# The first batch of an FFT filter takes the path of the later batches, through DRAM

## The chip, the cores and the metric

The kernel runs on one core of one Trainium2 chip. The metric is the device time of one execution in microseconds; the time given for a kernel is the median of its runs. TensorE multiplies matrices into PSUM, VectorE (DVE), ScalarE (ACT) and GpSimd (POOL) work elementwise, and nearly all transfers are issued by SyncE, whose queue (SPq) takes its instructions strictly in order.

## The reference

```python
X = np.fft.rfft(x, axis=1)                       # x: (8, 3072, 256) float32
y = np.fft.irfft(X * (filt_r + 1j*filt_i), n=3072, axis=1)
t = y.reshape(8*3072, 256)
h = np.maximum(t @ w_in, 0.0)                    # w_in (256, 2048), w_out (2048, 256): float64
z = h * h @ w_out
logits = z @ phi                                 # 32 slots = 8 experts x 4
slots = softmax(logits, over tokens).T @ z       # per expert: relu(slots @ w1) @ w2
out = softmax(logits, over slots) @ slots_out    # (24576, 256) float32
```

## The kernel before

The FFT of length 3072 is 128 x 24. Stage A multiplies the 128-point matrix with all of a batch (12 units of 128 x 512); its result S has to be regrouped, so that the 24-point matrices of stage B meet 24 values of one frequency block on the partitions. After stage B comes the filter (a complex product), then the inverse 24-point products, whose result G lies in DRAM. Each 512-token chunk is then read back from G (`gin`), takes the inverse 128-point product (line 408), is split in two halves of precision (`xo`, line 434) and goes through the pairs of the main loop: lines 468 to 470 multiply it with `wiH` and `wiL`, the two halves of w_in. There are 384 pairs, and TensorE is busy nearly all the time in them.

Work is ordered by hand. Each step is a function with a time, `put(t, fn)`; the times are only sort keys. Before the main loop there is a start stage: everything in `ev0`, sorted, fired in that order. In the main loop four streams (`dsp`, `late`, `fft`, `w`) are merged with the pairs by their times, so batches 1 to 7 transform beside the pairs of the batch before them.

Batches 1 to 7 use `fft_events`: S goes to DRAM (`S<-u`, 12 stores of 256 KB) and comes back regrouped in 8 rounds of two loads (`f<-S`, each 192 KB into 48 partitions, one at partition 0, one at 64). A round has 16 products of 48 x 32 by 256 (line 181; the trace counts them as 32), four VectorE products with the filter (line 192), four GpSimd sums (line 201), 16 inverse products (line 214), four copies out of PSUM on ScalarE (line 223) and two stores to G.

Batch 0 uses `start_events`. It keeps S on chip and regroups it by transfers from SBUF to SBUF: in each of 16 rounds two transfers `bi<-S` (line 324) read 4 partitions of S, 24 KB each, and write 96 partitions, 1 KB each. A round then has two 96 x 128 products (line 331), the filter in three VectorE operations and one sum, two inverse products (line 351), a copy (line 357) and a store `G<-go` (line 361). It has constants and a filter layout of its own (`fwf`, `ivf`, `pkf`), and half of each filter tile is copied from the other half on ScalarE (line 318).

The start stage also turns w_in, which comes as 8 float64 blocks, into `wiH` and `wiL`: per block a load `wt<-w_in`, a ScalarE copy (line 677), five VectorE operations (lines 649 to 654 and 688), a ScalarE copy to `wiH` (line 691) and a GpSimd difference `wiL` (line 693). Blocks of w_out are turned in the same way in the first pairs of the main loop. When the start stage ends, `open_main` gives its SBUF and PSUM to the main loop.

The framework gives SPq's transfers 8 completion semaphores in turn, so a transfer is not issued before the eighth before it has landed.

Of the kernel before, what the change touches and what calls it, by code (L numbers as in the profile page):

```python
# [38 lines left out]
def body(tc, x, cA, cAf, fwd, inv, flt, fwf, ivf, pkf, cst, w_in, w_out, phi, w1, w2, out):  # L39
# [26 lines left out]

    def groups(g):
        return [ST["B0"] + 1.2 + ST["dB"] * (g + k) for k in (0, 1, 1, 2, 3, 4, 5, 6)]

    WI = ((.35, conv_at(8.4, 0, SEQ, (4.2, 4.3))), (.55, conv_at(12.3, 0, SEQ, (5.6, 5.6))),  # L70
          (.75, conv_at(16.2, 0, SEQ, (4.2, 4.3))), (18.5, groups(0)), (28, groups(6)),
          (50.5, conv_at(59, 0, SEQ, (4, 4))), (52.7, conv_at(62.5, 0, SEQ, (4, 4))),
          (57, conv_at(66.2, 0, SEQ, (4, 4))))
    WO = [((64, 66.5, W)[n] if n < 3 else W + 2 * n - 4.5,
# [180 lines left out]


    def start_events(put, st):
        xv = x[0].rearrange("(p n) d -> p n d", n=N2)
        gv = st["G"].rearrange("(i t r) n d -> i (r n) t d", t=2, r=4)
        ca = first.tile([128, 128], F32, name="ca")  # L260
        S = first.tile([128, N2, D], F32, name="S")
        sv = S.rearrange("p n d -> p (n d)")

        wz = cv.tile([128, 512], F32, tag="wx", name="wz", bufs=1)

        def warm(a, n):

            p = side()
            w = a.shape[1]
            for _ in range(n):  # L270
                pe.matmul(p[:, 0:w], a[:, 0:128], a, start=True, stop=True)

        fb = [first.tile([128, 2048], F32, tag=f"fb{k}", name="fb") for k in range(4)]
        gps.memset(fb[3], 0.0)

        def load_ca():
            vec.memset(wz, 0.0)
            sync.dma_start(out=ca, in_=cAf)

        def load_x(sl):  # L280
            if sl % 2 == 0:
                st["x", sl // 2] = fb[sl // 2].rearrange("p (n d) -> p n d", d=D)
            a = 4 * (sl % 2)
            sync.dma_start(out=st["x", sl // 2][:, a:a + 4, :], in_=xv[:, 4 * sl:4 * sl + 4, :])

        def mm_a(u):
            p = side()
            a = 2 * (u % 4)
            pe.matmul(p, ca, st["x", u // 4][:, a:a + 2, :], start=True, stop=True)
            st["a", u] = p  # L290

        def evac_a(u):
            p = st.pop(("a", u))
            o = sv[:, 512 * u:512 * u + 512]
            act.activation(out=o, in_=p, func=ACTF.Copy)

        def load_w(q):
            w = first.tile([96, 4, 2, 128], F32, tag="fw", name="fwq", bufs=2)
            sync.dma_start(out=w, in_=fwf[q])
            st["fw", q] = w  # L300

        def load_v(q):
            w = first.tile([128, 4, 2, 96], F32, tag="iv", name="ivq", bufs=2)
            sync.dma_start(out=w, in_=ivf[q])
            st["iv", q] = w

        def load_f(h):

            f = fb[(h + 3) % 4].rearrange("p (i t c d) -> p i t c d", i=2, t=2, c=2)
            sync.dma_start(out=f[0:48], in_=pkf[2 * h:2 * h + 2, 0:48].rearrange("i p t c d -> p i t c d"))  # L310
            if h == 0:
                for k in range(2):
                    sync.dma_start(out=f[64:112, k, :, 0, :], in_=pkf[k, 64:112, :, 0, :])
            st["f", h] = f

        def copy_f(h):
            f = st["f", h]
            act.activation(out=f[64:112, :, :, 0, :], in_=f[0:48, :, :, 0, :], func=ACTF.Copy)

        def load_s(i):  # L320
            t = first.tile([96, 2, D], F32, tag="bi", name="bi", bufs=4)
            for tt in range(2):
# [2 lines left out]
            st["bi", i] = t

        def mm_b(i):
            t, c = st.pop(("bi", i)), st["fw", i // 4][:, i % 4]
            p = side()
            for tt in range(2):  # L330
                pe.matmul(p[:, tt * D:tt * D + D], c[:, tt, :], t[:, tt, :], start=True, stop=True)
            st["p", i] = p

        def filt(i):
            p = st.pop(("p", i)).rearrange("p (a d) -> p a d", d=D)
            f = st["f", i // 2][:, i % 2]
            u = first.tile([128, 2, D], F32, tag="u", name="u", bufs=2)
            v = first.tile([128, 2, D], F32, tag="v", name="v", bufs=2)
            vec.scalar_tensor_tensor(
                out=v[0:64], in0=p[64:128], scalar=-1.0, in1=f[0:64, :, 1, :], op0=ALU.mult, op1=ALU.mult  # L340
            )
            vec.tensor_tensor(out=v[64:128], in0=p[0:64], in1=f[0:64, :, 1, :], op=ALU.mult)
            vec.tensor_tensor(out=u, in0=p, in1=f[:, :, 0, :], op=ALU.mult)
            (gps if i < 14 else vec).tensor_tensor(out=u, in0=u, in1=v, op=ALU.add)
            st["y", i] = u

        def mm_g(i):
            y, c = st.pop(("y", i)), st["iv", i // 4][:, i % 4]
            p = side()
            for tt in range(2):  # L350
                pe.matmul(p[0:96, tt * D:tt * D + D], c[:, tt, :], y[:, tt, :], start=True, stop=True)
            st["g", i] = p

        def evac_g(i):
            p = st.pop(("g", i))
            o = first.tile([96, 2, D], F32, tag="go", name="go", bufs=3)
            act.activation(out=o, in_=p[0:96].rearrange("p (a d) -> p a d", d=D), func=ACTF.Copy)
            st["go", i] = o

        def store_g(i):  # L360
            sync.dma_start(out=gv[i], in_=st.pop(("go", i)))

        put(0, load_ca)
        put(0.05, warm, wz, 2)
        put(0.05, warm, wz[:, 0:256], 1)
        put(18.2, warm, ca, 16)
        for sl in range(6):
            put(0.1 * sl + 0.2, load_x, sl)
        for q in range(4):
            T = ST["B0"] + 4 * ST["dB"] * q  # L370
            put(0.8 if q == 0 else T - 6.5, load_w, q)
            put(1 if q == 0 else T - 1, load_v, q)
        for h in range(8):
            T = ST["B0"] + 2 * ST["dB"] * h
            put((1.1, 12.1, 19, 21)[h] if h < 4 else T - 7, load_f, h)
            if h:
                put(T - 0.5, copy_f, h)
        for u in range(12):
            put(4.6 + 0.9 * u, mm_a, u)
            put(6.7 + 1.0 * u, evac_a, u)  # L380
        for i in range(16):
            T = ST["B0"] + ST["dB"] * i
            put(max(T - 5, 18), load_s, i)
            put(T, mm_b, i)
            put(T + 1, filt, i)
            put(T + 5, mm_g, i)
            put(T + 6, evac_g, i)
            put(T + 9, store_g, i)
# [867 lines left out]
```

## Time and profile before

| what | value |
|---|---|
| median of 3 runs | 2188.33 us (2185.21 to 2192.13) |
| the profiled execution | 2184.73 us, span 2183.0 us |
| TensorE busy | 2068.9 us, 95% of the span |
| VectorE, ScalarE, GpSimd busy | 1391.4, 895.0, 848.4 us |
| mean granted TensorE clock | 0.968 of full speed |
| moved by DMA | 237.33 MB, mean 109 GB/s |

The span runs from the first to the last instruction of the profiled execution; 1.7 us of its time lie outside. Shares of busy time are means over a start stage, a long main loop and an end stage, which have different limits, so a stage is read in windows of its own.

### The profile page before, as it was taken

How to read it: one execution, taken by the hardware profiler on the slowest of the kernel's cores; microseconds unless marked ns; L12 is line 12 of the kernel's file. 1: busy time of each engine (PE TensorE's matmuls, PEld its weight loads, DVE VectorE, ACT ScalarE, POOL GpSimd, SP SyncE). 2: the span in 40 equal slices, each digit the busy share in tenths (PEclk: the TensorE clock that was granted, in tenths of full speed). 3: DMA queues.
4: the chain of work that ended last, by engine and by line, in shares of the span. 5: the costliest groups of instructions: out<-in, count | busy, mean ns of one | idle time of the engine just before them, and what ended most of it. 6: DMA issues, size and time to landing. Idle time of an engine off the chain costs nothing.

```text
span 2183.0 us, 43936 instructions
## 1 busy us (share of the span) xinstructions
PE 2068.9 (95%) x17950; PEld 1306.3 (60%) x17950; DVE 1391.4 (64%) x2534; ACT 895.0 (41%) x1771; POOL 848.4 (39%) x864
## 2 busy tenths in 40 slices
PE   6569999999999999999999999999999999999987
PEld 3346655665566656665666556656666556666556
DVE  3357666657665666666665666566666666666648
ACT  2134533443345333543345333533345334333335
POOL 2223543343334443543434433533435433332314
PEclk7569999999999999999999999999999999999999
DMA  6453453234314332242314331333324341300479
GB/s 173 114 158 107 143 128 94 77 116 105 95 45 139 93 99 65 96 126 77 100 53 131 98 106 47 114 108 80 97 67 133 99 108 46 109 23 12 129 251 386
DMA packets 142889, 237.33 MB, mean 109 GB/s; under 512 B 13344, under 2 KB 95840, under 8 KB 142688
## 3 DMA queue, kind: packets, MB, share of 16 engines
q1 hardware_dynamic: 142544, 234.39, 36.3%
q8 instruction: 141, 2.31, 0.5%
q14 instruction: 60, 0.49, 0.1%
q0 software_dynamic: 144, 0.13, 0.0%
HBM read 153.73 MB, written 77.59 MB: 106 GB/s over the span
## 4 chain that ended last, share of the span: by engine, by line
PE 84%; DMA 7%; DVE 5%; SPq 2%; issue 2%; ACT 1%; ACTq 0%; DVEq 0%
PE p L468 18%; PE p L470 15%; PE p L469 15%; PE sd L587 10%; PE L L496 8%; PE sd L408 4%; DMA bi<-S 3%; PE sd L181 3%; PE sd L214 2%; DMA f<-S 2%; PE sd L535 2%; DVE h L477 1%; PE sd L141 1%; PE sd L142 1%; PE sd L143 1%
## 5 line engine op out<-in xcount | busy, mean ns | idle before, releaser
L480 POOL TENSOR_TENSOR h<-h 128x512 f32<-128x512 f32 x384 | 399.7, 1041 | 961.6 <-ACT h L479 903.5
L468 PE MATMUL p<-xo,wiH 128*128 128x512 f32 x1536 | 669.3, 436 | 11.3 <-DVE h L477 8.5
L469 PE MATMUL p<-xo,wiH 128*128 128x512 f32 x1536 | 608.4, 396 | 0.9 <-POOL xo L434 0.9
L470 PE MATMUL p<-xo,wiL 128*128 128x512 f32 x1536 | 607.9, 396 | 0.0
L477 DVE SCALAR_TENSOR_TENSOR h<-p,h 128x512 f32<-128x512 f32 x384 | 264.2, 688 | 446.4 <-ACT h L476 446.4
L487 DVE STREAM_TRANSPOSE hT<-h 128x512 f32<-128x512 f32 x768 | 516.4, 696 | 15.5 <-POOL h L480 2.4
L468 PEld LDWEIGHTS p<-xo,wiH 128*128 128x128 f32 x1536 | 289.1, 188 | 258.4 <-issue 80.0
L479 ACT ACTIVATE h<-p 128x512 f32<-128x512 f32 x384 | 229.9, 599 | 432.3 <-PE p L470 427.7
L476 ACT ACTIVATE h<-p 128x512 f32<-128x512 f32 x384 | 228.7, 595 | 287.6 <-PE p L470 284.4
L470 PEld LDWEIGHTS p<-xo,wiL 128*128 128x128 f32 x1536 | 289.6, 189 | 70.0
L469 PEld LDWEIGHTS p<-xo,wiH 128*128 128x128 f32 x1536 | 290.4, 189 | 59.0 <-issue 9.8
L587 PE MATMUL sd<-hT,eT 32*32 32x512 f32 x6144 | 219.2, 602 | 4.4 <-DVE eT L566 2.9
L496 PE MATMUL L<-h,wf 128*32 128x512 f32 x1536 | 206.5, 607 | 0.8 <-POOL h L480 0.8
L201 POOL TENSOR_TENSOR u<-u 128x256 f32<-128x256 f32 x224 | 160.4, 738 | 107.3 <-DVE u L192 107.3
L192 DVE TENSOR_TENSOR u<-sd,f 128x512 f32<-128x512 f32 x224 | 142.8, 678 | 89.8 <-PE sd L181 89.6
L587 PEld LDWEIGHTS sd<-hT,eT 32*32 32x32 f32 x6144 | 106.2, 103 | 114.8 <-issue 57.7
L603 DVE SCALAR_TENSOR_TENSOR ac<-ac,sc,sd 128x512 f32<-128x512 f32 x188 | 133.9, 731 | 28.8 <-PE sd L587 28.8
L135 POOL TENSOR_TENSOR u<-f,u 128x512 fp32r<-128x512 f32 x84 | 108.2, 1289 | 75.4 <-ACT u L134 74.5
L408 PEld LDWEIGHTS sd<-cst_t,gin 128*128 128x128 f32 x768 | 98.1, 194 | 46.5 <-issue 21.0
L434 POOL TENSOR_TENSOR xo<-xt,xo 128x512 fp32r<-128x512 f32 x95 | 121.4, 1294 | 0.3 <-ACT xo L431 0.3
L408 PE MATMUL sd<-cst_t,gin 128*128 128x128 f32 x768 | 107.6, 284 | 2.3 <-DMA gin<-G 2.3
L418 ACT ACTIVATE xt<-sd 128x512 f32<-128x512 f32 x96 | 57.3, 597 | 118.6 <-PE sd L408 118.6
(120 smaller groups left out, 1663.0 us busy)
## 6 DMA issues: line engine op xcount, KB each, us to landing
f<-flt SPq DMA_DIRECT2D x56, 512.0 KB
gin<-G SPq DMA_DIRECT2D x48, 512.0 KB
out<-w1t SPq DMA_DIRECT2D x47, 512.0 KB
f<-x SPq DMA_DIRECT2D x42, 512.0 KB
S<-u SPq DMA_DIRECT2D x84, 256.0 KB
f<-S SPq DMA_DIRECT2D x112, 192.0 KB
G<-f SPq DMA_DIRECT2D x112, 192.0 KB
wx<-w SPq DMA_DIRECT2D x34, 256.0 KB
```

Source lines behind the costliest of these rows:

```text
L201: gps.tensor_tensor(out=a[:, h, :], in0=a[:, h, :], in1=b[:, 1 - h, :], op=ALU.add if h else ALU.subtract)
L408: pe.matmul(p[:, 128 * a:128 * a + 128], t[:, a, 128 * k:128 * k + 128], cI, start=True, stop=True,)
L468: pe.matmul(p, wh, x[:, 0, kk, :], start=(kk == 0), stop=False)
L469: pe.matmul(p, wh, x[:, 1, kk, :], start=False, stop=False)
L470: pe.matmul(p, wl, x[:, 0, kk, :], start=False, stop=(kk == 1))
L476: act.activation(out=h, in_=p, func=ACTF.Relu, scale=2.0 ** -16)
L477: vec.scalar_tensor_tensor(out=h, in0=p, scalar=0.0, in1=h, op0=ALU.max, op1=ALU.mult)
L479: act.activation(out=h, in_=p, func=ACTF.Relu, scale=2.0 ** -8)
L480: gps.tensor_tensor(out=h, in0=h, in1=h, op=ALU.mult)
L487: vec.transpose(hT[c][:, 2 * i + k, :], h2[P, k])
L496: pe.matmul(lg[c][32 * n:32 * n + 32, :], wf[:, f, :], h2.pop((P + n // 2, n % 2)), start=(f < 4), stop=(f >= FT - 4), tile_position=(0, 3 ...
L587: pe.matmul(S[r][32 * t:32 * t + 32, :], e[rows, o:o + 32], h[rows, :, o:o + 32], start=(a == 0), stop=(a == 3), tile_position=(32 * r, 32 ...
```

## The change

Batch 0 now calls `fft_events` too. It has a branch `b == 0`: stage A keeps its single full-precision product per unit (the later batches split x in two halves first) and its ScalarE copy, then stores S to DRAM; the 8 rounds are those of the later batches. Its tiles come from the pool `first`, with 17 buffers of 4 KB per partition (`f4`: x, filter, S and G tiles), 12 of 2 KB (`u`) and 4 of the constants; the later batches have 5, 8 and 2. The sort keys of the start stage are new: the w_in blocks are spread over the stage, a round's loads stand rounds ahead of it. `start_events`, its constants and its filter layout are gone. In every batch `fw` is now loaded by two transfers into 48 partitions each instead of one into 128. The load of `ca_t` (used by batch 1 on) moves from the start to the middle of the rounds.

```diff
-    ST = dict(B0=20.5, dB=2.2, G0=66, Gd=1.5)
+    ST = dict(B0=22, dB=4, G0=58.5, Gd=1.5)
...
+    WI = [(t, conv_at(c, 0, SEQ, (1, 1.5))) for t, c in (
+        (.9, 14), (12.1, 19), (24.2, 29.2), (28.2, 35.2), (34.2, 41.2), (40.2, 47.2), (46.2, 53.2), (52.2, 58.2)
+    )]
...
         def mm_a(u):
+            p = side()
+            if b == 0:
+                a = 2 * (u % 2)
+                pe.matmul(p, st["ca"], st["x", u // 2][:, a:a + 2, :], start=True, stop=True)
+                st["a", u] = p
+                return
...
         def load_c(i):
-            w = G["fft"].tile([128, 4, 2, 32], F32, tag="fw", name="fw", bufs=2)
-            sync.dma_start(out=w, in_=fwd[i])
+            w = pl().tile([128, 4, 2, 32], F32, tag="fw", name="fw", bufs=n["c"])
+            for r in range(2):
+                sync.dma_start(out=w[64 * r:64 * r + 48], in_=fwd[i, 64 * r:64 * r + 48])
...
+        if b == 0:
...
+            for sl in range(6):
+                put(0.1 * sl + 0.2, load_x, sl)
+            for u in range(12):
+                put(4.6 + 0.9 * u, mm_a, u)
+                put(6.7 + 1.0 * u, evac_a, u)
+            for i in range(8):
+                T = ST["B0"] + ST["dB"] * i
+                put((.7, .75, 15)[i] if i < 3 else T - 6.5, load_c, i)
+                put((.8, 9, 15.5)[i] if i < 3 else T - 6.4, load_f, i)
+                put(18 + .1 * i if i < 3 else T - 6, load_s, i)
+                put(T, mm_b, i)
+                for r in range(2):
+                    put(T + 1 + .5 * r, filt, i, r)
+                    put(T + 1 + .5 * r, join, i, r)
+                put(T + 5, mm_g, i)
+                for c in range(4):
+                    put(T + 6, evac_g, i, c)
+                put(T + 7, store_g, i)
+            return
...
-    def start_events(put, st):
...
-        def load_s(i):
-            t = first.tile([96, 2, D], F32, tag="bi", name="bi", bufs=4)
-            for tt in range(2):
-                r = 8 * i + 4 * tt
-                sync.dma_start(out=t[:, tt, :], in_=S[r:r + 4])
...
-        put0(54, load_const)
-        start_events(put0, st)
+        put0(38, load_const)
+        fft_events(0, lambda: first, put0, 0, 0, 0, 0, dict(f=17, u=12, c=4), st)
```

The first place is SyncE's queue in the middle of the start stage. Before, two consecutive rounds had these rows (`bi` are the regrouped tiles, `go` the results, `fb` the filter; in brackets the semaphores waited for):

```order
L324 DMA bi<-S 96x1x256 [waits DMAHW2_49,PE_49]
L324 DMA bi<-S 96x1x256 [waits DMAHW3_49]
L361 DMA G<-go 96x2x256 [waits DMAHW4_49,Activation_49]
L324 DMA bi<-S 96x1x256 [waits DMAHW5_49,PE_49]
L324 DMA bi<-S 96x1x256 [waits DMAHW6_49]
L310 DMA fb<-pkf 48x2x1024 [waits DMAHW7_49,DVE_49]
L299 DMA fwq<-fwf 96x1024 [waits DMAHW0_49]
L361 DMA G<-go 96x2x256 [waits DMAHW1_49,Activation_49]
```

Now one round there has these (`f_423` is round 4's regrouped tile, `f_416` its filter, `f_338` and `f_418` the results of rounds 0 and 1):

```order
L233 DMA G<-f_338 48x4x256 [waits DMAHW7_49,Activation_49]
L233 DMA G<-f_338 48x4x256 [waits DMAHW0_49]
L159 DMA fw<-fwd 48x256 [waits DMAHW1_49,PE_49]
L159 DMA fw<-fwd 48x256 [waits DMAHW2_49]
L161 DMA iv<-inv 128x256 [waits DMAHW3_49,PE_49]
L166 DMA f_416<-flt 128x1024 [waits DMAHW4_49]
L172 DMA f_423<-S 48x4x256 [waits DMAHW5_49]
L172 DMA f_423<-S 48x4x256 [waits DMAHW6_49]
L233 DMA G<-f_418 48x4x256 [waits DMAHW7_49,Activation_49]
```

Before, a regrouping transfer waited for TensorE, which had to free its buffer; now the loads of round 4 stand behind the store of round 0 and wait for no engine.

The second place is VectorE late in the start stage. Before, one operation of a w_in block (lines 649 and following) stood between the filter operations of two rounds:

```order
L339 SCALAR_TENSOR_TENSOR v<-sd,fb 64x512
L342 TENSOR_TENSOR v<-sd,fb 64x512
L343 TENSOR_TENSOR u<-sd,fb 128x512
L653 TENSOR_SCALAR we<-wa 128x512
L339 SCALAR_TENSOR_TENSOR v<-sd,fb 64x512
```

Now four filter operations of a round are followed by the five of a whole block; here the last round (`f_644`) and the first operations of block 6 behind it:

```order
L193 TENSOR_TENSOR u<-sd,f_644 128x512 [waits DMAHW0_49,PE_49,Pool_49]
L193 TENSOR_TENSOR u<-sd,f_644 128x512 [waits Pool_49]
L193 TENSOR_TENSOR u<-sd,f_644 128x512 [waits PE_49]
L193 TENSOR_TENSOR u<-sd,f_644 128x512
L555 TENSOR_SCALAR wa<-wa 128x512 [waits Activation_49]
L556 SCALAR_TENSOR_TENSOR wa<-wt,wa 128x512 [waits DMAHW5_49,DVE_49]
```

Of the eight blocks two now stand ahead of the first round on VectorE, four between the rounds and two behind the last.

The third place is ScalarE at the end of the start stage, where each row with `wiH` waits for VectorE's block and the copies of a round's result stand behind it. It was, for the last two rounds:

```order
L357 ACTIVATE go<-sd 96x512 [waits DMAHW3_49,PE_49,Activation_49]
L677 ACTIVATE wa<-wt 128x512 [waits DMAHW0_49,Pool_49]
L357 ACTIVATE go<-sd 96x512 [waits DMAHW6_49,PE_49,Activation_49]
L677 ACTIVATE wa<-wt 128x512 [waits DMAHW2_49,Pool_49]
L691 ACTIVATE wiH<-wa 128x512 [waits DVE_49]
```

It is now, for the last round (`f_814` is its result tile):

```order
L583 ACTIVATE wa<-wt 128x512 [waits DMAHW5_49,Pool_49]
L597 ACTIVATE wiH<-wa 128x512 [waits DVE_49]
L224 ACTIVATE f_814<-sd 128x256 [waits DMAHW4_49,PE_49]
L224 ACTIVATE f_814<-sd 128x256 [waits PE_49] x3
L583 ACTIVATE wa<-wt 128x512 [waits DMAHW0_49,Pool_49]
```

The copies of the last result now stand behind `wiH` of block 6.

## Rows read from the trace of the kernel before

**Rows 1.** The page, part 1: span and busy time (instructions) of each engine.

```profile
span 2183.0 us, 43936 instructions
...
PE 2068.9 (95%) x17950; PEld 1306.3 (60%) x17950; DVE 1391.4 (64%) x2534; ACT 895.0 (41%) x1771; POOL 848.4 (39%) x864
```

**Rows 2.** Start stage in windows: length, busy (count) per engine, PEclk, DMA share, GB/s.

```profile
0.00:5.00 5.00, 3.54 (x4) 1.51 (x5) 0.48 (x1) 1.28 (x1) 2.74 (x6) 1.00 0.59 171
5.00:10.00 5.00, 5.00 (x11) 2.13 (x9) 0.18 (x1) 1.96 (x4) 0.00 (x0) 1.00 1.03 385
10.00:15.00 5.00, 4.70 (x12) 1.96 (x12) 4.32 (x8) 4.21 (x8) 1.07 (x1) 1.00 1.03 404
25.00:30.00 5.00, 1.64 (x3) 0.94 (x4) 0.00 (x0) 0.00 (x0) 0.00 (x0) 0.50 0.24 57
131.00:137.00 6.00, 4.80 (x15) 2.88 (x14) 3.82 (x6) 3.15 (x6) 0.00 (x0) 0.76 1.07 381
```

**Rows 3.** The chain that ended last, from 24 to 131 us: shares by line.

```profile
by line: DMA bi<-S 66.0%; PE sd L331 11.6%; SPq L310 7.3%; SPq L324 6.6%; PE sd L351 4.4%; SPq L361 2.6%; SPq L299 2.1%; issue 1.8%; SPq L304 0.6%
```

**Rows 4.** Line 331's products: what TensorE waited for (us, times).

```profile
  DMA bi<-S: 80.7, 43
```

**Rows 5.** The timeline from 139 to 151 us: start, length, engine, line [idle before].

```profile
140.19 0.34 SPq L394 DMA_DIRECT2D gin<-G  x1
...
144.30 3.56 PE L408 MATMUL sd<-cst_t,gin 128*128 128x128 f32 x16 [2.32 <-DMA gin<-G]
...
149.06 0.50 PE L468 MATMUL p<-xo,wiH 128*128 128x512 f32 x1 [1.21 <-ACT xo L431]
```

**Rows 6.** Transfers of later batches in windows, columns as in Rows 2.

```profile
477.00:478.00 1.00, 1.00 (x33) 0.51 (x18) 0.15 (x1) 0.24 (x1) 1.00 (x2) 1.00 0.97 384
478.00:480.00 2.00, 2.00 (x9) 1.32 (x7) 1.81 (x3) 0.60 (x1) 2.00 (x2) 1.00 0.94 180
489.00:498.00 9.00, 8.22 (x64) 4.53 (x62) 6.08 (x11) 3.84 (x8) 3.94 (x5) 1.00 0.90 232
600.40:602.40 2.00, 2.00 (x12) 1.67 (x11) 1.42 (x3) 1.12 (x2) 0.00 (x0) 1.00 0.66 173
```

**Rows 7.** SyncE's queue in batch 2's rounds: start, length, line, transfer.

```profile
475.35 0.86 SPq L171 DMA_DIRECT2D f<-S  x2
488.08 0.79 SPq L232 DMA_DIRECT2D G<-f  x2
...
599.33 15.85 SPq L232 DMA_DIRECT2D G<-f  x4
617.68 0.34 SPq L394 DMA_DIRECT2D gin<-G  x1
```

**Rows 8.** One round's products, then lines 192, 201, 223 (ns min/median/max) and 181's waits.

```profile
476.66 1.09 PE L181 MATMUL sd<-f,fw 48*32 48x256 f32 x32
...
L192 DVE TENSOR_TENSOR u<-sd,f x224: 650/680/693, 262.8 to 1821.1; 128x512 f32<-128x512 f32 x112
...
L201 POOL TENSOR_TENSOR u<-u x224: 722/738/778, 264.1 to 1823.2; 128x256 f32<-128x256 f32 x112
...
L223 ACT ACTIVATE f<-sd x224: 377/384/408, 272.2 to 1827.5; 128x256 f32<-128x256 f32 x112
...
  DMA f<-S: 5.3, 8
```

**Rows 9.** The timeline from 9 to 23 us: operations of w_in blocks.

```profile
9.82 0.43 DVE L649 TENSOR_SCALAR wa<-wa 128x512 uint32<-128x512 uint32 x1 [8.41 <-ACT wa L677]
10.28 0.69 DVE L650 SCALAR_TENSOR_TENSOR wa<-wt,wa 128x512 uint32<-128x512 uint32 x1
...
12.19 0.69 DVE L688 TENSOR_TENSOR wa<-wa,we 128x512 f32<-128x512 f32 x1
...
13.93 1.70 POOL L693 TENSOR_TENSOR wiL<-wa,wiH 128x512 fp32r<-128x512 f32 x1 [10.15 <-ACT wiH L691]
14.54 1.37 DVE L653 TENSOR_SCALAR we<-wa 128x512 uint32<-128x512 uint32 x1
...
22.65 0.63 ACT L691 ACTIVATE wiH<-wa 128x512 fp32r<-128x512 f32 x1 [2.65 <-DVE wa L688]
```

More of the change, by code (lines that the diff above doesn't have):

```diff
@@ L36, with body @@
 C_END = 420
-def body(tc, x, cA, cAf, fwd, inv, flt, fwf, ivf, pkf, cst, w_in, w_out, phi, w1, w2, out):
+def body(tc, x, cA, cAf, fwd, inv, flt, cst, w_in, w_out, phi, w1, w2, out):
     nc = tc.nc
@@ L65, in body @@
     SEQ = (.5, .6, .7, .8, .9)
[L67 to L74, printed above, removed]
+    WI = [(t, conv_at(c, 0, SEQ, (1, 1.5))) for t, c in (
+        (.9, 14), (12.1, 19), (24.2, 29.2), (28.2, 35.2), (34.2, 41.2), (40.2, 47.2), (46.2, 53.2), (52.2, 58.2)
+    )]
+    WO = [((56.5, 57, W)[n] if n < 3 else W + 2 * n - 4.5,
            [W + max(2 * n + k - 1.5, 0) for k in (-1, -.5, 0, .5, 1, 1.5, 2, 2.5, 3.5, 4)]) for n in range(8)]
@@ L114, in done, with fft_events @@
             free.append(taken.pop(id(p))[0])
-    def fft_events(b, G, put, A0, dA, B0, dB, n, st):
+    def fft_events(b, pl, put, A0, dA, B0, dB, n, st):
         xv = x[b].rearrange("(p n) d -> p n d", n=N2)
         def big():
-            return G["fft"].tile([128, 4, D], F32, tag="f4", name="f4", bufs=n["f"])
+            return pl().tile([128, 4, D], F32, tag="f4", name="f4", bufs=n["f"])
         def small():
-            return G["fft"].tile([128, 2, D], F32, tag="u", name="u", bufs=n["u"])
+            return pl().tile([128, 2, D], F32, tag="u", name="u", bufs=n["u"])
         def load_x(sl):
@@ L156, in load_c @@
         def load_c(i):
-            w = G["fft"].tile([128, 4, 2, 32], F32, tag="fw", name="fw", bufs=2)
-            sync.dma_start(out=w, in_=fwd[i])
-            v = G["fft"].tile([128, 2, 2, 64], F32, tag="iv", name="iv", bufs=2)
+            w = pl().tile([128, 4, 2, 32], F32, tag="fw", name="fw", bufs=n["c"])
+            for r in range(2):
+                sync.dma_start(out=w[64 * r:64 * r + 48], in_=fwd[i, 64 * r:64 * r + 48])
+            v = pl().tile([128, 2, 2, 64], F32, tag="iv", name="iv", bufs=n["c"])
             sync.dma_start(out=v, in_=inv[i])
@@ L232, in store_g, with load_ca, warm @@
                 sync.dma_start(out=gv[i, r], in_=o[64 * r:64 * r + 48])
+        def load_ca():
+            vec.memset(st["wz"], 0.0)
+            sync.dma_start(out=st["ca"], in_=cAf)
+        def warm(a, n):
+            p = side()
+            w = a.shape[1]
+            for _ in range(n):
+                pe.matmul(p[:, 0:w], a[:, 0:128], a, start=True, stop=True)
+        if b == 0:
+            st["wz"] = cv.tile([128, 512], F32, tag="wx", name="wz", bufs=1)
+            st["ca"] = pl().tile([128, 128], F32, name="ca")
+            put(0, load_ca)
+            put(0.05, warm, st["wz"], 2)
+            put(0.05, warm, st["wz"][:, 0:256], 1)
+            put(18.2, warm, st["ca"], 16)
+            for sl in range(6):
[17 more added lines that the diff above has]
+            return
         for sl in range(6):
@@ L254, in fft_events @@
             put(T + 5.5, store_g, i)
-    def start_events(put, st):
[L258 to L318, printed above, removed]
-        def load_s(i):
-            t = first.tile([96, 2, D], F32, tag="bi", name="bi", bufs=4)
-            for tt in range(2):
-                r = 8 * i + 4 * tt
-                sync.dma_start(out=t[:, tt, :], in_=S[r:r + 4])
[L325 to L388, printed above, removed]
@@ L807, in load_const @@
     def load_const():
+        gps.dma_start(out=ca_t, in_=cA)
         sync.dma_start(out=cst_t, in_=cst)
@@ L838, in body @@
         put, late = stream("fft"), stream("late")
-        gps.dma_start(out=ca_t, in_=cA)
-        st = {"G": dram.tile([N1, N2, D], F32, tag="G", name="G")}
-        put0(54, load_const)
-        start_events(put0, st)
+        st = {}
+        put0(38, load_const)
+        fft_events(0, lambda: first, put0, 0, 0, 0, 0, dict(f=17, u=12, c=4), st)
         out_events(0, st, late)
@@ L1205, in _lay_filter @@
     return np.ascontiguousarray(pk.reshape(8, 128, 4, D))
-def _pack_filter(fr, fi, ks):
-    import numpy as np
-    pk = np.zeros((32, 128, 2, D), np.float32)
-    for h in range(2):
-        for jj in range(2):
-            rows = slice(64 * h + 24 * jj, 64 * h + 24 * jj + 24)
-            pk[:, rows, 0, :] = fr[ks[jj::2]]
-            pk[:, rows, 1, :] = fi[ks[jj::2]]
-    pk[0, 64, 0, :] = fr[N // 2]
-    pk[0, 0, 1, :] = 0.0
-    pk[0, 64, 1, :] = 0.0
-    return np.ascontiguousarray(pk.reshape(16, 2, 128, 2, D).transpose(0, 2, 1, 3, 4))
 def kernel(**inputs):
@@ L1226 @@
     from concourse.bass_utils import run_bass_kernel_spmd
-    (cA, cAf, fwd, inv, fwf, ivf), cst, ks = _constants()
+    (cA, cAf, fwd, inv), cst, ks = _constants()
     arrays = {
@@ L1235 @@
         "flt": _lay_filter(inputs["filt_r"], inputs["filt_i"], ks),
-        "fwf": fwf,
-        "ivf": ivf,
-        "pkf": _pack_filter(inputs["filt_r"], inputs["filt_i"], ks),
         "cst": cst,
```

7 lines of the change are left out of this document (2 added, 5 removed).

## The prediction

> **What bounds the kernel now.** The page first [rows 1]: TensorE is busy 2068.9 of 2183.0 us, so the main loop is bound by TensorE, and the loop's instructions don't change. What can change is the time before the first product of the main loop. The timeline gives it: line 468 starts at 149.06 us [rows 5]. From there to the end of the execution are 2184.7 - 149.1 = 2035.7 us, which I leave as they are.
>
> Then the windows of the start stage [rows 2]. The reader is to see three regimes. While x is loaded, DMA moves 385 to 404 GB/s with every engine busy (share 1.03). In the rounds it falls to 57 GB/s at a share of 0.24, about 4 of 16 DMA engines, and no compute engine is busy for half of that window. At the end of the stage, when G is stored and w_in loaded and nothing is regrouped, it is back at 381 GB/s. So the DMA engines are not short of capacity; the regrouping transfers use only a quarter of them. The chain of waits from 24 to 131 us says the same: 66% of it is the landing of `bi<-S` [rows 3], and TensorE waited for these 80.7 us in 43 waits [rows 4]. 32 transfers of 98 KB at 57 GB/s are 55 us, and the filter and constants stand in the same queue behind them.
>
> **The change, part by part.** It removes the regrouping on chip, 16 rounds, the half copies of the filter on ScalarE, and adds a trip of S through DRAM and 8 rounds of another form. I follow the new stage to the first main product, in four terms.
>
> *Term 1, S complete in DRAM.* The last of the 12 S stores stands on SyncE behind 9.67 MB, itself counted: x 3.15, S 3.15, three filter tiles 1.57, two w_in blocks 1.05, constants of three rounds 0.69, the first matrix 0.07. The first 5 us bring 171 x 5 = 0.86 MB; the other 8.81 MB at 385 GB/s take 22.9 us, so the bytes are through at 27.9, at 404 GB/s at 26.8 [rows 2]; 27.4 is between. A store's receipt: in batch 2 the last G store was issued by 599.33 + 15.85 = 615.18 and the `gin` that waits for it at 617.68, 2.5 us with 1.1 us of transfer (197 KB at 180 GB/s), so 1.4 us [rows 6, 7]. S is there at 28.8. Nothing before shows ScalarE holding up these stores, but two w_in blocks now stand among its 12 copies; from below that costs nothing (the queue of bytes is longer), from above one block, 2.9 us on VectorE, worked out below. I take nothing.
>
> *Term 2, the first round.* Two loads are issued in 0.86 us [rows 7], 393 KB at 180 GB/s take 2.2 us [rows 6], receipt 1.4, products 1.09 us at full clock [rows 8], 2.2 at the half clock that these idle stretches were granted (0.50, [rows 2]). VectorE starts at 28.8 + 0.9 + 2.2 + 1.4 + 2.2 = 35.5.
>
> *Term 3, eight rounds.* Two limits. VectorE: 8 x 4 x 0.68 = 21.8 us [rows 8], and four w_in blocks before the last round's filter ends, each 2 x 0.43 + 3 x 0.69 = 2.93 us [rows 9], 11.7. An operation of a block that meets a GpSimd one waits for it: line 653 took 1.37 us instead of 0.43 beside `wiL` [rows 9]. One such per block, 0.9 to 1.0 us, adds 4. VectorE alone would end the last filter at 35.5 + 37.5 = 73. DMA: from S's completion to the last S load 10.97 MB stand in order, of which S loads 3.15, four rounds' G stores 1.57 and `fw` 0.49 go to or from 48 partitions, 5.21 together, and 5.76 go to all 128 (filters 2.62, w_in 2.10, `iv` 0.66, constants of later stages 0.38). When only S loads or G stores were left in the queue, it moved 180 and 173 GB/s; when a filter tile was under way, 384; a mixture of both 232 [rows 6]. At 180 and 384 the sum is 28.9 + 15.0 = 43.9 us, the last S load is there at 29.7 + 43.9 + 1.4 = 75, and with its products and filter, 2.2 + 2.7, the stage is at 80. At 384 for all it would be 28.6 us and VectorE the limit. I take 76.5, halfway between 73 and 80, since a full queue lets the two halves and the wide transfers overlap in part, which no row isolates.
>
> [...]
>
> *Term 4, to the first main product.* Behind the last filter stands w_in block 6 on VectorE, 2.93 + 1.0; beside it run the last sums (two of 0.74 after the filter) and inverse products (2.2 at half clock), 3.7 together. ScalarE has `wiH` of that block (0.63, [rows 9]) ahead of the four copies, 4 x 0.384 [rows 8]. Then two stores, 0.79, landing 2.5 [rows 7]: 76.5 + 3.9 + 0.6 + 1.5 + 0.8 + 2.5 = 85.8. From the issue of `gin` to line 468 the old stage took 149.06 - 140.19 = 8.9 us [rows 5], with the same instructions. The first main product is at 94.7.
>
> *The rest.* Prefetch: round i + 4's loads stand behind round i's store, which waits for ScalarE, so each load has two rounds to land. GpSimd's sums are 8 x 4 x 0.74 = 24 us beside VectorE's 37.5. The second `fw` transfer of each later round costs SyncE some 0.4 us, 56 times; the queue has gaps of tens of us between rounds, and TensorE waited for S loads only 5.3 us in all of batches 1 to 7 [rows 8]; without that cover it would be 22 us at most. `ca_t` is needed only by batch 1. Both at nothing.
>
> *Sum.* 149.1 - 94.7 = 54.4 us less: 2184.7 - 54.4 = 2130.3 for the profiled execution. That one was 3.6 us below the median of the three runs, so 2188.3 - 54.4 = 2134 for a median.
>
> **The rivals.** *VectorE sets the pace, transfers hidden.* For it: 381 GB/s with G stores in the queue [rows 2]. Then the last filter ends at 69 to 73 and the main loop starts at 87 to 91: 2126 to 2130; with S there 1.4 us earlier, 2124. *Transfers set it all the way.* For it: 232 GB/s over nine us of a real mixture [rows 6]. 10.97 MB are then 47.3 us, the last S load is there at 78, and 3.1 MB stand behind it (four G stores, two w_in and one w_out block), 13.6 us more, so the main loop starts at 78 + 13.6 + 2.5 + 8.9 = 103: 2142; at 180 for everything 2150. Against it: the mixture was measured with gaps of issue in it. *Slower: each round waits for its trip.* If the loads of a round in fact wait for the store of the round before, a round is 0.9 + 2.2 + 1.4 (load) + 2.2 + 2.7 + 1.5 + 2.2 + 1.5 + 0.8 (store) = 15.4 us, eight are 123, and the main loop starts at 28.8 + 123 + 11.4 = 163: 2202. It decides from 13.6 us per round. Against it: the order of SyncE's queue and 17 buffers. *No gain: the loop gives it back.* The old stage's 55 us could return as later waits for S loads; they would have to grow from 5.3 us tenfold [rows 8]. Nothing shows why.
>
> **How the numbers follow.** The forecast, a start of the main loop between 89 and 101, has 0.52: 2134, with 2128 to 2140 its own range. VectorE alone 0.24, transfers all the way 0.17, trip per round 0.04, no gain 0.03. A median of this kernel tells 0.3%, 6.6 us, from no change. Faster is the sum of the first three, 0.93; the same 0.03; slower 0.04. The range 2119 to 2150 holds the first three cases nearly whole; its lower end leaves 5 us below the VectorE case for overlaps that I count in line.
>
> **What would show it.** Right: line 468 starts near 95 us; windows of the rounds show over 200 GB/s and a DMA share above 0.7; VectorE is busy most of the time between 35 and 77; the first product of a round starts near 33. Term 1 is wrong if the first S load is issued before 27 or after 32. Term 3 is wrong if waits of TensorE for S loads in the rounds are long (transfers) or absent (VectorE). Wrong altogether: rounds over 13.6 us apart, or a main loop longer than 2036 us.

## The result and the profile after

The changed kernel took 2138.55 us (median of 4 runs, 2135.92 to 2141.19), the kernel before 2186.77 us beside it (4 runs, 2185.17 to 2192.13). The ratio is 0.9775 with a 95% interval of 0.9751 to 0.9799, so 48.2 us less (44.0 to 54.5). The forecast was 2134 us, 54.4 us less. The profiled execution of the changed kernel took 2136.33 us.

The page, part 1, answers to [rows 1]:

```profile
span 2134.5 us, 44755 instructions
...
PE 2047.0 (96%) x18334; PEld 1288.3 (60%) x18334; DVE 1375.0 (64%) x2516; ACT 888.0 (42%) x1780; POOL 851.3 (40%) x881
```

The span is 48.5 us shorter, and TensorE's busy time only 21.9 us: more than half of what went is time in which it did nothing. The start stage in windows, with the columns of [rows 2]:

```profile
5.00:10.00 5.00, 5.00 (x12) 2.54 (x11) 0.00 (x0) 1.86 (x4) 0.00 (x0) 1.00 1.02 389
10.00:15.00 5.00, 5.00 (x13) 2.21 (x12) 0.00 (x0) 2.92 (x5) 0.00 (x0) 1.00 1.04 329
15.00:20.00 5.00, 5.00 (x36) 4.04 (x35) 2.34 (x5) 1.16 (x2) 0.00 (x0) 1.00 1.02 377
20.00:25.00 5.00, 0.33 (x3) 0.14 (x2) 1.01 (x2) 2.75 (x5) 1.26 (x1) 0.88 1.06 385
...
35.00:45.00 10.00, 9.67 (x158) 3.79 (x142) 5.91 (x10) 1.77 (x5) 5.52 (x8) 0.54 1.09 245
45.00:55.00 10.00, 6.35 (x96) 2.75 (x96) 9.79 (x16) 3.34 (x10) 7.26 (x9) 0.80 1.04 305
55.00:65.00 10.00, 8.71 (x112) 3.03 (x96) 5.91 (x10) 2.55 (x7) 5.00 (x7) 0.51 1.04 267
65.00:75.00 10.00, 7.82 (x95) 3.32 (x96) 9.77 (x15) 3.60 (x10) 7.57 (x9) 0.66 1.02 302
```

The rounds now have DMA shares above 1.0 and 245 to 305 GB/s. The 0.24 and 57 GB/s of [rows 2] are a window with almost nothing but regrouping; over the old rounds as a whole, filters and constants among them, the kernel before had 0.43 and 105 GB/s:

```profile
40.00:131.00 91.00, 53.56 (x107) 28.23 (x108) 32.59 (x48) 15.25 (x21) 18.96 (x14) 0.52 0.43 105
```

In the changed kernel VectorE is busy nearly all of two windows (9.79 and 9.77 of 10 us) and 5.91 us of the other two. The chain of waits from 30 to 98 us, by line, answers to [rows 3]:

```profile
by line: DMA f<-S 20.5%; PE sd L215 13.7%; DMA G<-f 12.8%; DVE u L193 7.6%; DMA gin<-G 7.5%; DMA S<-u 6.9%; PE sd L182 5.4%; issue 5.4%; ACT f L224 4.9%; PE sd L314 3.7%; DVE wa L556 3.3%; DVE we L560 2.7%; SPq L172 2.4%; DVE wa L555 2.1%;
```

The landing of the regrouped S was 66% of the chain and is now a fifth of a shorter one, and the rest is spread over transfers and engines. The timeline, against [rows 5] at its end (the main loop's first line is now 374, `gin` is issued by line 300):

```profile
30.11 2.77 SPq L172 DMA_DIRECT2D f<-S  x6
...
61.13 1.21 ACT L224 ACTIVATE f<-sd 128x256 f32<-128x256 f32 x4 [3.89 <-PE sd L215]
...
62.20 0.69 ACT L583 ACTIVATE wa<-wt 128x512 f32<-128x512 f32 x1
...
62.93 0.43 DVE L555 TENSOR_SCALAR wa<-wa 128x512 uint32<-128x512 uint32 x1 [3.96 <-ACT wa L583]
...
69.88 3.19 PE L215 MATMUL sd<-u,iv 32*64 32x256 f32 x28
...
73.12 2.51 PE L182 MATMUL sd<-f,fw 48*32 48x256 f32 x32
...
74.89 0.69 DVE L594 TENSOR_TENSOR wa<-wa,we 128x512 f32<-128x512 f32 x1
...
75.76 2.48 DVE L193 TENSOR_TENSOR u<-sd,f 128x512 f32<-128x512 f32 x4 [0.17 <-PE sd L182]
...
83.54 1.19 ACT L224 ACTIVATE f<-sd 128x256 f32<-128x256 f32 x4
...
84.75 0.80 SPq L233 DMA_DIRECT2D G<-f  x2
...
88.83 0.34 SPq L300 DMA_DIRECT2D gin<-G  x1
...
97.68 0.80 PE L374 MATMUL p<-xo,wiH 128*128 128x512 f32 x1 [1.20 <-ACT xo L337]
```

The first main product starts at 97.68 instead of 149.06 us, 51.4 earlier. The rows at 61 to 63 us show a wait that the prediction does not name: VectorE stands still for 3.96 us, because the copy that opens a w_in block (line 583) stands on ScalarE behind the four copies of a round (line 224), and these wait for the round's last inverse products. The waits from 30 to 90 us (total, times, longest) give the sum of such waits, and what is left of TensorE's wait for S loads [rows 4]:

```profile
DVE wa L555 <- ACT wa L583: 9.9, 4, 4.0
...
PE sd L182 <- DMA f<-S: 0.5, 2, 0.3
```

Of the 9.9 us, 2.44 and 3.96 lie in the rounds, together 6.4; the other two, 1.20 and 2.34 us, come behind the last filter, before the last two w_in blocks.

### The profile page after: what moved, and what is told of

Same layout as the page of the kernel before. It is cut to its first block, busy times and chain, and to the rows that moved or that the text cites. A ratio compares the mean times of both kernels' runs of the same rounds, so it can differ in the third digit from the quotient of the medians.

```text
span 2134.5 us, 44755 instructions
## 1 busy us (share of the span) xinstructions
PE 2047.0 (96%) x18334; PEld 1288.3 (60%) x18334; DVE 1375.0 (64%) x2516; ACT 888.0 (42%) x1780; POOL 851.3 (40%) x881
## 4 chain that ended last, share of the span: by engine, by line
PE 87%; DVE 6%; DMA 3%; issue 2%; ACT 1%; SPq 1%; POOL 0%; DVEq 0%; ACTq 0%
PE p L374 19%; PE p L375 15%; PE p L376 15%; PE sd L493 10%; PE L L402 9%; PE sd L314 4%; PE sd L182 3%; PE sd L215 3%; PE sd L441 2%; DMA f<-S 2%; DVE u L193 1%; PE sd L141 1%; DVE ac L509 1%; PE sd L142 1%; DVE h L383 1%
## 5 line engine op out<-in xcount | busy, mean ns | idle before, releaser
L393 DVE STREAM_TRANSPOSE hT<-h 128x512 f32<-128x512 f32 x768 | 516.4, 696 | 15.4 <-POOL h L386 2.1
L202 POOL TENSOR_TENSOR u<-u 128x256 f32<-128x256 f32 x256 | 184.3, 743 | 117.5 <-DVE u L193 117.5
L193 DVE TENSOR_TENSOR u<-sd,f 128x512 f32<-128x512 f32 x256 | 162.5, 678 | 100.9 <-PE sd L182 100.6
L224 ACT ACTIVATE f<-sd 128x256 f32<-128x256 f32 x256 | 79.8, 388 | 84.7 <-PE sd L215 84.7
```

The costliest lines, as they stand in the source:

```text
L193: vec.tensor_tensor(out=u, in0=p.rearrange("p (h d) -> p h d", d=D), in1=f[:, 2 * r + k:2 * r + k + 1, :].to_broadcast([128, 2, D]), op=AL ...
L202: gps.tensor_tensor(out=a[:, h, :], in0=a[:, h, :], in1=b[:, 1 - h, :], op=ALU.add if h else ALU.subtract)
L393: vec.transpose(hT[c][:, 2 * i + k, :], h2[P, k])
```

## The experiments

All are read by the start of the first main product; "rest" is the time of that execution less this start. Each row is one execution. In e7, e10 and e11, whose kernels are three lines longer there, line 374 is line 377.

| run | first main product, us | time, us | rest, us |
|---|---|---|---|
| before | 149.06 | 2184.73 | 2035.7 |
| changed kernel | 97.68 | 2136.33 | 2038.7 |
| the same again | 96.62 | 2137.33 | 2040.7 |
| e1_dram_old_rounds | 98.31 | 2136.17 | 2037.9 |
| e9_dram_four_rows | 121.55 | 2154.82 | 2033.3 |
| e2_load_behind_store | 169.23 | 2207.42 | 2038.2 |
| e3_pool_6 | 100.87 | 2141.30 | 2040.4 |
| e4_copy_ahead | 100.75 | 2136.59 | 2035.8 |
| e5_last_copies_first | 95.93 | 2138.30 | 2042.4 |
| the same again (e5_again) | 98.59 | 2143.89 | 2045.3 |
| e7_filter_reused | 95.87 | 2140.81 | 2044.9 |
| e8_all_three | 99.24 | 2136.21 | 2037.0 |
| e10_both_lifted | 92.49 | 2136.28 | 2043.8 |
| e11_lifted_old_copies | 96.45 | 2136.88 | 2040.4 |

Two kernels have two rows: their starts differ by 1.1 and 2.7 us. A difference below 3 us between two rows is not read as an effect, and one of 3 to 4 us only with care.

**Which part of the change carries the gain.** The kernel before, with only the place of S changed:

```diff
+            if u == 0:
+                st["Sd"] = dram.tile([N1, N2, D], F32, tag="S", name="S")
+            sync.dma_start(out=st["Sd"].rearrange("p n d -> p (n d)")[:, 512 * u:512 * u + 512], in_=o)
...
-                sync.dma_start(out=t[:, tt, :], in_=S[r:r + 4])
+                sync.dma_start(out=t[:, tt, :], in_=st["Sd"][r:r + 4].rearrange("r n d -> (r n) d"))
```

> The kernel before with one part of the change alone: S is stored to DRAM in 12 stores and each bi tile is loaded from there (two loads of 24 x 4 rows into 96 partitions), the 16 rounds, buffers and order stay. My theory (regrouping from 4 partitions used a quarter of the DMA engines and set the pace): the 3.15 MB of regrouping take 3.15 / 0.18 = 17 us instead of 55, the S stores add 3.15 / 0.385 = 8 us ahead of them, so line 468 moves from 149.1 us to 115 to 125, a time near 2155. Rival (the old rounds' shallow buffers and order on SyncE set the pace): line 468 stays above 140 us.

Windows of this run; `bi` is issued from 32.45 us, the share is 0.00 from 32.5 to 33.0 and 0.10 from 33.0 to 33.5; the next other transfer is issued at 34.23, so the first row is read as `bi` alone:

```profile
34.00:34.50 0.50, 0.00 (x0) 0.00 (x0) 0.00 (x0) 0.00 (x0) 0.00 (x0) 0.50 0.71 184
...
50.00:55.00 5.00, 3.70 (x17) 2.44 (x16) 4.85 (x8) 2.56 (x5) 3.00 (x2) 1.00 1.11 256
```

The tile view of `bi`, what TensorE waited for (us, times), against [rows 4]:

```profile
  DMA bi<-S: 24.0, 9
```

And the timeline at the main loop's first product:

```profile
98.31 0.80 PE L471 MATMUL p<-xo,wiH 128*128 128x512 f32 x1 [1.21 <-ACT xo L434]
```

With the old 16 rounds, the old buffers and the old order, the start is 50.8 us earlier than before and 0.6 us behind the changed kernel. The source of the regrouping is the change; the rounds of the later batches, the deep pool and the order by need add nothing that single executions can tell.

**What makes the DRAM source fast.** As e1, but DRAM rows padded by 256 values, so that a transfer's source can't be merged to 96 rows and stays 4 x 24 x 256:

```diff
-                st["Sd"] = dram.tile([N1, N2, D], F32, tag="S", name="S")
+                st["Sd"] = dram.tile([N1, N2 + 1, D], F32, tag="Sp", name="S", bufs=1)
...
-                sync.dma_start(out=t[:, tt, :], in_=st["Sd"][r:r + 4].rearrange("r n d -> (r n) d"))
+                sync.dma_start(out=t[:, tt, :], in_=st["Sd"][r:r + 4, 0:N2, :])
```

> The run e1_dram_old_rounds again, S in DRAM, with one thing changed: the copy in DRAM has rows of 25 x 256 instead of 24 x 256, so that the source of a bi transfer can't be one run of 96 rows and stays 4 x 24 x 256, as it was on chip. Same bytes, same 1 KB pieces, same order. My theory (the number of DMA engines follows from the outermost count, 4, wherever the source lies): a share near 0.25 and 50 to 70 GB/s in the rounds again, line 468 at 145 to 165 us. Rival (transfers out of 4 partitions of SBUF are slow as such): as in e1_dram_old_rounds, line 468 near 99 us.

Windows at the start of the rounds (`bi` is issued from 32.23 us, the share is 0.00 from 32.5 to 33.5; the next other transfer is issued at 35.08):

```profile
34.50:35.00 0.50, 0.00 (x0) 0.00 (x0) 0.00 (x0) 0.00 (x0) 0.00 (x0) 0.50 0.21 74
35.00:35.50 0.50, 0.00 (x0) 0.00 (x0) 0.00 (x0) 0.00 (x0) 0.00 (x0) 0.50 0.23 82
...
33.50:36.00 2.50, 0.00 (x0) 0.00 (x0) 0.00 (x0) 0.00 (x0) 0.00 (x0) 0.50 0.23 59
...
60.00:70.00 10.00, 6.68 (x19) 4.26 (x17) 4.79 (x8) 2.94 (x4) 3.77 (x3) 0.66 0.65 169
```

And the tile view of `bi`:

```profile
  DMA bi<-S: 50.6, 30
```

Neither theory alone. The form of the source, with the same bytes from the same DRAM, sets the share of these transfers: 0.23 with 4 outer rows, 0.71 with 96. It is worth 121.55 - 98.31 = 23.2 us. The other 149.06 - 121.55 = 27.5 come with moving the source from 4 SBUF partitions to DRAM, and by what is not shown. With regrouping alone in the queue the share is the same, 0.24 and 0.23, and the rates are not clearly apart: 57 GB/s from SBUF over 5 us [rows 2]; from DRAM 59 over 2.5 us with the slow first one, 74 and 82 in the half microseconds shown. Among the other transfers e9 moved more, 169 GB/s at a share of 0.65 from 60 to 70 us against 105 at 0.43 over the rounds of the kernel before, which restates the gain and does not explain it.

Counted as engines, the mean shares of 0.24 and 0.23 with 4 outer rows are 3.8 and 3.7 of 16, near the 4 of the theory; the 0.71 of e1 with 96 is 11, more than 4 but not 16. That a source in 4 partitions of SBUF has a limit of its own is not shown: the 57 GB/s of [rows 2] stand beside 59 to 82 GB/s in e9, at nearly the same share without a source in SBUF, so some four engines may account for much of it, and no row shows how many transfers were in flight.

**The rival on the slower side.** The changed kernel with each round's load behind the store of the round before (and rounds twice as far apart in the sort keys, the blocks of w_in and w_out with them):

```diff
-    ST = dict(B0=22, dB=4, G0=58.5, Gd=1.5)
+    ST = dict(B0=22, dB=8, G0=87, Gd=1.5)
...
-                put(18 + .1 * i if i < 3 else T - 6, load_s, i)
+                put(18 if i == 0 else T - .9, load_s, i)
```

> The changed kernel with each round's S loads put behind the G store of the round before, rounds apart (no prefetch). My theory, and the price of the slower rival of the prediction: a round is a full trip, 15.4 us by the sum there, so line 374 starts near 160 us and the time is near 2200, above that of the kernel before. Rival (a trip costs little because loads land in 5 us and engines are idle anyway): rounds under 10 us, line 374 before 125 us.

SyncE's queue:

```profile
60.27 0.79 SPq L233 DMA_DIRECT2D G<-f  x2
61.11 1.46 SPq L172 DMA_DIRECT2D f<-S  x2
...
76.75 0.83 SPq L233 DMA_DIRECT2D G<-f  x2
...
93.23 0.83 SPq L233 DMA_DIRECT2D G<-f  x2
```

Rounds are 16.5 us apart and the kernel takes 25 us more than the one before beside it (2182.31). So with these eight rounds the gain needs a round's load to be issued ahead of the store of the round before.

**How deep.** The changed kernel with `f=6` in place of `f=17`.

> The changed kernel with 6 tiles of 4 KB in batch 0's pool instead of 17, nothing else. My theory (prefetch needs the tiles): loads of round 3 wait for the filter of rounds 0 and 1 and everything on SyncE waits behind them, rounds of 9 to 12 us, line 374 at 115 to 130 us. Rival (depth is not needed, the order alone does it): line 374 within 3 us of the 97.7 us of the changed kernel.

The theory of a deep pool is wrong: the start, 100.87 us, is far from 115 to 130. It is 3.2 and 4.3 us later than the two rows of the changed kernel, so some cost of the small pool is likely but not told for sure.

**What limits the new rounds.** Fewer transfers (batch 0's rounds 3 to 7 take the filter tiles of rounds 0 to 2, so another filter is applied there):

```diff
+            if b == 0 and i > 2:
+                st["f", i] = st["f", i % 3]
+                return
```

> The changed kernel with the filter tiles of rounds 3 to 7 of batch 0 not loaded: rounds 3 to 7 multiply with those of rounds 0 to 2 (this changes what batch 0 computes). 2.62 MB less are moved. My theory after the traces (VectorE and the order on ScalarE set the pace of the rounds, transfers land just in time): line 374 starts within 2 us of 97.7 us. Rival (transfers set the pace, the term of the prediction): 2.62 MB at 300 GB/s, 8 to 9 us earlier, near 89 us.

ScalarE's order (the copy of blocks 2, 4 and 6 ahead of a round's copies in one run, `wiH` of block 6 behind the last copies in another):

```diff
-    WI = [(t, conv_at(c, 0, SEQ, (1, 1.5))) for t, c in (
+    WI = [(t, conv_at(c, -2 if n in (2, 4, 6) else 0, SEQ, (1, 1.5))) for n, (t, c) in enumerate((
```

```diff
+    WI = [(t, conv_at(c, 0, SEQ, (3.3, 3.6) if n == 6 else (1, 1.5))) for n, (t, c) in enumerate((
```

> The changed kernel with the ScalarE copy (line 583) of w_in blocks 2, 4 and 6 put ahead of a round's four copies instead of behind them. My theory (VectorE waited 2.4, 4.0 and 1.2 us for these copies, and VectorE sets the pace): line 374 starts 4 to 7 us earlier, at 91 to 94 us. Rival (round 3's S load lands at 46 us whatever VectorE does, so transfers take over at once): within 2 us of 97.7 us.

> The changed kernel with wiH of w_in block 6 put behind the last round's four ScalarE copies. My theory (the last products end at 81.7 us and their copies begin at 83.5, behind wiH): line 374 starts 1.5 to 2 us earlier, near 96 us. Rival (what is still queued on the DMA engines delays the last G stores anyway): no change.

And both, with less ahead of the first S load:

```diff
-                put((.7, .75, 15)[i] if i < 3 else T - 6.5, load_c, i)
-                put((.8, 9, 15.5)[i] if i < 3 else T - 6.4, load_f, i)
+                put((.7, .75, 18.3)[i] if i < 3 else T - 6.5, load_c, i)
+                put((.8, 18.15, 18.35)[i] if i < 3 else T - 6.4, load_f, i)
```

> Both edits of e4_copy_ahead and e5_last_copies_first, and the filters of rounds 1 and 2 and the constants of round 2 loaded behind the first S load instead of ahead of the S stores. My theory for the third (S is complete when all bytes ahead of it are through, 1.28 MB less at 385 GB/s): the first S load is issued at 26.5 to 27.5 us instead of 30.1, and with all three line 374 starts at 87 to 91 us. Rival (ScalarE's copies of the last units, ended at 22.7 us behind a w_in block, set it): the first S load stays at 29 to 30 us and line 374 comes no earlier than with the other two.

From e4_copy_ahead a row of its waits, and one of the timeline, VectorE in the last rounds:

```profile
ACT wa L583 <- DMA wt<-w_in: 13.3, 2, 12.8
...
70.44 1.89 DVE L193 TENSOR_TENSOR u<-sd,f 128x512 f32<-128x512 f32 x3 [4.82 <-PE sd L182]
```

The chain of waits of e8_all_three (start, us, what):

```profile
28.23 5.30 DMA f<-S
33.55 8.10 DMA wt<-w_in
...
52.78 7.11 DMA f<-flt
59.91 3.65 DMA fw<-fwd
```

e7 is 1.8 us earlier than the changed kernel, where 2.62 MB at the 300 GB/s of the rounds would be 8.7; its last S load landed at 70.65 us instead of 73.59. e4 is 3.1 later, outside both expectations: ScalarE's copy now waits for the w_in block to land, the waits of 2.44 and 3.96 us on VectorE are gone, and one of 4.82 us for a round's products stands in their place. e5 was 1.75 us earlier, as expected, and 0.9 later in its second execution, so it tells nothing. In e8 the first S load is issued 3.2 us earlier (26.89), as its bytes say, and nothing of it reaches the end: the chain goes through the landings of w_in, filter and constants. Each limit lifted by itself shows another one. The theory that this leaves, two limits of nearly equal length, was put to the test by lifting both:

> The kernel of e8_all_three (w_in copies ahead of a round's copies, block 6's copy behind the last round's, filters 1 and 2 behind the first S load) in which rounds 3 to 7 of batch 0 also reuse the filter tiles of rounds 0 to 2: 2.62 MB less, and the filter applied to those frequencies is another one. Theory (two limits of nearly equal length, VectorE with ScalarE's order on one side and transfers on the other, and each single edit only showed the other): with both lifted VectorE starts at 33, runs 32 operations of 0.62 and four blocks of 3.9, and the last filter ends near 70; 17.7 from there to the first main product as in e5, so 87 to 90. Rival (a third limit, such as the chain TensorE, VectorE, GpSimd, TensorE of a round, or the receipts of transfers): the first main product stays at 95 or later.

> e10_both_lifted with the w_in copies of blocks 2 and 4 back behind a round's copies on ScalarE. Theory (ScalarE's order holds VectorE up by 9.9 us in the rounds once transfers don't): VectorE starts 3.4 earlier than in the changed kernel and keeps its idle time, so the first main product is at 95.9 - 3.4 = 92.5, 3 to 5 us behind e10_both_lifted. Rival (the copies' place costs nothing by itself, VectorE was waiting for something that would have been late anyway): the same as e10_both_lifted within 1 us.

e10 starts the main loop at 92.49, 3.4 us ahead of any other row, while its parts alone gave +1.6 (e8) and -1.8 (e7). That fits limits that cover each other; with single executions up to 2.7 us apart it is not more than that. The theory's 87 to 90 was too early: VectorE ended its last filter at 75.5, not 70. The trace shows why:

```profile
42.35 0.66 ACT L586 ACTIVATE wa<-wt 128x512 f32<-128x512 f32 x1 [15.00 <-DMA wt<-w_in]
...
43.04 0.43 DVE L558 TENSOR_SCALAR wa<-wa 128x512 uint32<-128x512 uint32 x1 [5.09 <-ACT wa L586]
```

VectorE waited 5.09 us for a copy, and the copy for its w_in block to land, so transfers were not out of the way there. e11 is 4.0 us behind e10, in the expected 3 to 5. But its edit puts back the copy of block 6 as well as those of blocks 2 and 4, its copy of block 2 waits for the landing too (until 43.95), and its last filter ends only 1.5 us behind e10's (76.92). What the place of the copies costs by itself is not shown.

**Where the early start goes.** e10 started 5.2 us earlier than the changed kernel and took the same time, 2136.28 against 2136.33. Counted by the 1536 products of this line, e10 leads by 8.3 us at the 701st, by 3.9 at the 751st and by 1.5 at the 901st. TensorE's timeline in e10 between the 701st and the 751st:

```profile
993.81 2.59 PE L185 MATMUL sd<-f,fw 48*32 48x256 f32 x32 [2.85 <-DMA fw<-fwd]
```

Windows of the same place:

```profile
990.00:993.20 3.20, 0.96 (x3) 0.48 (x3) 1.27 (x2) 0.60 (x1) 1.28 (x2) 0.96 1.09 235
993.20:1000.00 6.80, 6.19 (x44) 2.33 (x45) 2.62 (x4) 0.60 (x1) 1.42 (x2) 0.52 0.67 167
```

The same round in the timeline of the changed kernel:

```profile
999.88 0.59 PE L182 MATMUL sd<-f,fw 48*32 48x256 f32 x2 [0.60 <-issue]
1000.73 1.09 PE L182 MATMUL sd<-f,fw 48*32 48x256 f32 x30 [0.26 <-DMA f<-S]
```

And its windows:

```profile
998.00:1001.20 3.20, 2.33 (x26) 1.05 (x31) 1.56 (x3) 0.68 (x2) 1.61 (x2) 1.00 1.01 252
1001.20:1008.00 6.80, 6.80 (x51) 4.08 (x36) 5.12 (x8) 1.79 (x3) 3.42 (x5) 1.00 0.60 161
```

In these two places a round's load comes late while DMA has a share of 1.09 and 1.01. Where TensorE waits 0.9 us in all, the granted clock stays at 1.00; where it waits 2.85, it is 0.52 over the next 6.8 us, and the round's products take 2.59 us for 32 instead of 1.09 for 30. The length of the wait alone does not decide it, as two other batches of the changed kernel show (rows of timeline and windows):

```profile
756.79 0.59 PE L182 MATMUL sd<-f,fw 48*32 48x256 f32 x2 [1.20 <-DMA f<-S]
...
757.60:761.00 3.40, 3.33 (x33) 1.58 (x33) 1.29 (x2) 0.00 (x0) 0.00 (x0) 0.50 0.94 273
...
1242.87 0.59 PE L182 MATMUL sd<-f,fw 48*32 48x256 f32 x2 [2.04 <-issue]
...
1243.00:1250.00 7.00, 6.61 (x57) 3.86 (x56) 4.48 (x7) 1.34 (x3) 2.30 (x3) 1.00 0.70 197
```

A wait of 1.20 us was followed by 3.4 us at a granted clock of 0.50, one of 2.04 us by 7 us at 1.00. Such stretches lie at different batches in the two executions: from 993.2 to 1000 and from 1239 to 1245.8 us (0.52 both) in e10, where the changed kernel had 1.00, and in the changed kernel from 515.5 to 519 (0.54) and from 757.6 to 761 (0.50). With the starts they are what I can name of the rest's spread between 2033 and 2045 us, in which a start some us earlier is lost.

**Timed.** Two kernels again, beside 11 runs of the kernel before (median 2188.04):

> The kernel of e5_last_copies_first, timed: the copy of w_in block 6 stands behind the last round's copies. If the 1.75 us that it saved before the main loop stay saved, its median is 1 to 3 us below that of the changed kernel in the same call, which is within what this measurement can tell; if the loop takes them back, as it took 3 us back in the changed kernel, the two are equal.

> The changed kernel, unaltered, timed beside the others: 2136 to 2141 us, a ratio of 0.975 to 0.980 to the kernel before.

e5's kernel took 2140.61 us (5 runs), 0.9783 of before (0.9759 to 0.9808); the changed kernel 2142.60 (6 runs), 0.9794 (0.9769 to 0.9819). The changed kernel's median was above the expected 2136 to 2141, its ratio inside 0.975 to 0.980. The 2.0 us between the two kernels are of the expected size, 1 to 3, but the intervals overlap nearly whole: no version was shown to be faster than the changed kernel.

## Why the prediction was right

*What bounds the start.* Right, and e1 and e9 show it: the low DMA share (0.24; 0.23 with the same form in DRAM, 0.71 with 96 rows there) came from the regrouping transfers' form and source, and changing only these is the gain. The 57 GB/s at 0.24 were not the whole of the old rounds, which had 105 at 0.43. The part of the change to which half of the working goes, eight rounds of another form, is worth nothing measurable.

*Term 1.* 28.8 us for S, measured 30.11 for its first load. The bytes were right (e8: 1.28 MB fewer ahead of it, and 3.2 us earlier). The rate was not 385 to 404 all the way: 329 GB/s from 10 to 15 us make some 0.8 of the 1.3 us, an estimate (5 us at 65 GB/s less than 394), and 377 and 385 in the next two windows most of the rest.

*Term 2.* 35.5, measured 36.62: the delay of term 1 handed on.

*Term 3.* 76.5, measured 75.76 + 2.48 = 78.24. From VectorE's start that is 41.6 us against 41.0 predicted, and that they lie so near is luck. I took VectorE's own 37.5 and added half of the way to a limit by transfers, 3.5. VectorE's own work was 35.1, which is 41.6 less waits of 6.4 and 0.2 us: four filter operations took 2.48, not 2.72 us. And the waits on it were 2.44 and 3.96 us for ScalarE's copy behind the round's copies, an order that I had costed only for the last block; for S loads TensorE waited 0.5 us. By the sign that the prediction names, waits absent, VectorE would be the limit; but that sign misses a load that lands while TensorE is still busy, and transfers were close behind: the last S load, put at 75 by the slow rates, landed at 73.59. The last filter began at 75.76, when VectorE's block had ended at 75.58 and the round's products at 75.63; these had begun at 73.12, when TensorE's products of line 215 ended (73.07) and half of the load had landed (73.03). So limits of VectorE, TensorE and transfers met within some 0.2 us, and this trace does not tell which one set the end. In e7, with the last S load 2.9 us earlier, the last filter ended at 76.91, 1.3 us earlier.

The rounds moved 245 to 305 GB/s, 280 in the mean of the four windows, between the 232 and the 381 of [rows 2, 6]. That a full queue lets the two halves (the transfers of 48 partitions at 0 and at 64) and the wide transfers overlap in part, the reason for the 3.5 us, was my assumption; no run here moved the halves apart.

*Term 4.* `gin` at 85.8, measured 88.83: 1.7 us handed on from term 3, 1.2 because block 6 waits for its copy, 0.8 because the stores land in 3.3 instead of 2.5 us, less 0.7 by which block and copies were shorter. From there 8.9 predicted, 8.85 measured.

*The rest.* Taken as unchanged; 2038.7 against 2035.7 in the profiled executions. TensorE's waits for S loads in batches 1 to 7 went from 5.3 [rows 8] to 6.3 us (us, times):

```profile
  DMA f<-S: 6.3, 7
```

So the rival "the loop gives it back" has no case. The 3 us are within the 12 us over which the rest varies; that they come from the change is not shown. The start late by 3.0 and the longer rest by 3.0 are the 6.0 us between 2136.33 and the 2130.3 forecast for a profiled execution.

*Rivals.* VectorE alone would have started the main loop at 87 to 91 us, transfers all the way at 103; it started at 97.7. The price of the second at 180 GB/s for everything was summed wrong: 10.97 MB are then 60.9 us and 3.1 MB 17.2, which makes 2160 and not 2150, so the stated range held less of that rival than the text says. The slower one, a trip in each round, was sized at 15.4 us per round and 2202 us; built as e2, it took 16.5 us and 2207. It did not occur because the S loads do stand ahead of the stores in SyncE's queue and wait for no engine, as the order showed (those of `fw` and `iv` of the same round do wait for TensorE).

## What to carry to other kernels

A DMA share well below 1 with the same few transfers in the queue can be a limit of their form (here 0.24, and 0.23 with 4 outer rows in DRAM against 0.71 with 96): look at the outermost dimension of the source and at whether it lies in a few partitions (leaving 4 of them for DRAM came with 27.5 us here, not taken apart), and try a copy in DRAM whose rows merge before rebuilding the loop around it. Two limits of nearly equal length can hide each other (here the start moved by +1.6 and -1.8 us with one side lifted and by -5.2 with both, single executions that fit this), so an edit that moves one alone says little; lift both in one kernel, and profile one kernel twice first to know what a difference between single executions is worth.
